# Reordering the second half-chunk of an attention + gated-MLP kernel: copies before masks, transposes and sums in twos

## The chip, the cores and the metric

The kernel runs on one core of a Trainium2 chip. The metric is the device time of one execution in microseconds (us), median of the runs shown. Beside it stands one execution taken by the hardware profiler, from which all durations in this document come. Engines are named as in the profile: PE (TensorE matmuls), PEld (TensorE weight loads), DVE (VectorE), ACT (ScalarE), POOL (GpSimd), SP (SyncE, which here only issues DMAs).

## What is computed

Attention with 4 batches, 8 heads, 768 positions and head dimension 64, followed by a gated MLP on 3072 tokens (512 to 1536 to 512). A query attends to the first 8 positions (global) and to the last 96 (local), with a bias that falls with the distance by a slope of its head:

```python
scores = scale * np.matmul(q, k.transpose(0, 1, 3, 2))
...
keep = is_global | is_local
dist = np.where(is_global & ~is_local, float(n_local), np.abs(rel).astype(np.float32))
slopes = 2.0 ** (-8.0 * (np.arange(H, dtype=np.float32) + 1) / H)
bias = -slopes[:, None, None] * dist[None, :, :]
scores = np.where(keep, scores + bias, -1000000000.0)
a = softmax(scores)
x = (a @ v), heads side by side, one row per token
out = (np.maximum(x @ w_gate, 0.0) * (x @ w_val)) @ w_out
```

(The softmax and the last two lines are shortened here.)

## The kernel before

**Half-chunks.** The work is cut into 8 half-chunks `s` of 384 queries (batch `s // 2`, half `s % 2`), and the 8 heads into 4 pairs `p`. A half-chunk has two parts: attention, which leaves a normalised `xT` (512 features by 384 tokens), and the MLP on it (`ffn_pieces`, L525 to L569). Half-chunks 0 and 1 are written out by hand, order and all (L621 to L734); later ones are woven (`weave`, L588), with attention of the next half-chunk between the MLP products of this one. The order that the code is written in is the order of each engine's queue, since scheduling is manual. This case concerns half-chunk 1 ("the second half", L690 to L734).

**Attention of a pair.** `piece_t` (L299) transposes the pair's keys and queries on PE into a PSUM bank of the pool `av_ps` (2 banks); in half-chunk 1 its matmuls fill 64 columns of the array each. `piece_copy` has DVE copy the result out: the keys in three instructions (L282, L283, L284), the queries in two (L315). Then scores are made on PE in three banks of the pool `qk_ps` (3 banks), in one of two ways:

- by bias (`piece_bias` L327, `piece_scores` L342, `piece_exp` L359): PE adds the distance bias as matmuls with `sid` and `dd`, and ACT takes the exp of a bank into an `es` buffer. Nothing is left for DVE.
- by mask (`piece_qk` L411): PE makes bare scores, ACT takes the exp (L414), and DVE multiplies the result by a ready-made mask exp(-slope x distance) (L423, five instructions for a pair in this half). The masks `m_all` are built per head by ACT (`setup_mask`, L245).

Half-chunk 0 uses the bias for all pairs; half-chunk 1 uses it for pairs 0 and 3 and the mask for pairs 1 and 2. An `es` buffer is one of three in rotation; for the last pair of half-chunk 0 the unused tile `kN` serves instead.

**Sums.** `piece_av_wide` (L474) makes, for a pair, the sums of the weights (with a matrix of ones) and the weighted sums of V, each with matmuls of 64 columns for one head and the other beside it. ACT takes Ln (L491) and Exp of its negative (L496) as the inverse, and DVE multiplies into `xT` (L502). `AV(s, p)` is all of this for one pair. It takes two PSUM banks, from `av_ps` or where named from another pool.

**V rows.** The 8 global V rows are copied on DVE beside each of the seven V tiles (`copy_v_globals`, L145): tiles 1 to 3 in half-chunk 0, tiles 4 to 6 in half-chunk 1.

**MLP.** `gate(fc)` is four matmuls of 384 columns (L525) into a bank of the pool `ff_ps` (3 banks, in rotation) and a relu on ACT (L534); `val(fc)` is four matmuls and a multiplication on DVE into `ht` (L541). While half-chunk 1's attention is made, gates and vals of half-chunk 0 are placed between its parts. Weights come by DMAs that POOL issues (L166), some of them while this goes on; POOL also issues the loads of q and k for half-chunk 2 (L111).

The order of half-chunk 1 before the change, from L690 on: transposes, copies and biased scores of pairs 0 and 1 as far as the copies; masks of heads 2 and 3; three gates; then `S1(1)` (QK, exps and masks of pair 1), masks 4 and 5, V rows 4 to 6, transposes and copies of pair 2, gate 3, transposes and copies of pair 3, val 0, `S1(2)`, val 1, sums of pair 0, bias and scores of pair 3, val 2, sums of pair 1, val 3, sums of pair 2, gate 4, sums of pair 3, val 4, gate 5, val 5. In this text val and gate with a number mean the block `fc`; the next product after val 5 is the first gate of half-chunk 1 ("chunk 1").

Of the kernel before, what the change touches and what calls it, by code (L numbers as in the profile page):

```python
# [15 lines left out]
def kernel(  # L16
# [21 lines left out]
    HP = H // 2  # L38
# [6 lines left out]
    NT = -(-S // KT)  # L45
# [43 lines left out]
    kNb = [const.tile([128, HP, QH], BF16, name=f"kN{i}") for i in range(2)]  # L89
# [53 lines left out]
    def copy_v_globals(eng, b, j0, j1):  # L143
        t = vbuf[b % 2][0:NG, :, D:].rearrange("p j (h z) -> p j h z", z=2 * D)[:, :, :, 0:D]
        eng.tensor_copy(t[:, j0:j1], t[:, 0:1].to_broadcast([NG, j1 - j0, H, D]))  # L145
# [98 lines left out]
    def setup_mask(h):  # L244
        nc.scalar.activation(m_all[:, h], dd, AF.Exp, bias=0.0, scale=-slopes[h])  # L245
# [42 lines left out]
    def piece_t(s, p, pool=av_psum, name="av_ps", apart=False):  # L288
        for i in (1, 0):
            if i == 1 or apart:  # L290
                tp = pool.tile([128, 512], FP32, name=name)
                tp = tp[:, 0:QH].bitcast(BF16).rearrange("d (i t) -> d i t", i=2)
            tp_of[s, p, i] = tp[:, i, :]
            for n in range(NN):
                for e in range(2 if s == 1 else 1):
                    r = slice(64 * e, 64 * e + 64) if s == 1 else slice(0, 128)
                    src = (qk16[s, i][:, 2 * p + e, n * D : (n + 1) * D] if s == 1
                           else cast_of[s, p][:, i, n])
                    nc.tensor.matmul(tp[r, i, n * 128 : (n + 1) * 128],  # L299
                                     lhsT=src, rhs=ident, is_transpose=True,  # L300
                                     start=((i == 1 or apart) and n == 0),
                                     stop=((i == 0 or apart) and n == NN - 1))

    def piece_copy_k(s, p):
        b, half = divmod(s, 2)
        put_keys(nc.vector.tensor_copy, nc.vector.tensor_copy, kT[b % 2][p], tp_of[s, p, 1], half)

    def piece_copy(s, p):
        piece_copy_k(s, p)
        piece_copy_q(s, p)  # L310
# [8 lines left out]
    def piece_bias(s, p):  # L319
        pool, name = (ff_psum, "ff_ps") if s == 0 and p % 2 else (qk_psum, "qk_ps")  # L320
        banks = [pool.tile([128, 512], FP32, name=name) for _ in range(3)]
        qk_of[s, p] = banks
        for g, bank in enumerate(banks_of_half[s % 2]):
            c = 0
            for i, (j, a, w, m) in enumerate(bank):
                for e in range(2):
                    nc.tensor.matmul(banks[g][:, c : c + NN * w], lhsT=sid[:, 2 * p + e],  # L327
                                     rhs=dd[:, 0 if j == 0 else 1, :, m : m + w],
                                     start=(i == 0 and e == 0), stop=False, skip_group_check=True)
                    c += NN * w  # L330
# [13 lines left out]
                c += n_  # L344

    def piece_exp(s, p, g):
        if s == 0 and p == HP - 1:

            es = kNb[0].rearrange("d p t -> d (p t)")[:, 480 * g : 480 * (g + 1)]
        else:  # L350
            if g == 0:
                es01_of[s, p] = es_pool.tile([128, 2, 480], BF16, name="es01")
            es = es01_of[s, p][:, g] if g < 2 else es_pool.tile([128, 480], BF16, name="es2")
        c = 0
        for j, a, w, m in banks_of_half[s % 2][g]:
            for e in range(2):
                es_of[s, p, j, e] = (es, c)
                c += NN * w
        nc.scalar.activation(es[:, 0:c], qk_of[s, p][g][:, 0:c], AF.Exp, bias=0.0, scale=scale)  # L359

    def piece_biased(s, p):
        piece_scores(s, p)
        for g in range(3):
            piece_exp(s, p, g)
# [30 lines left out]
        out += [(0.0, lambda p=p: piece_order(s, p)) for p in range(HP)]  # L395
        return out

    def piece_qk(s, p, g):
        b, half = divmod(s, 2)
        kt = kT[b % 2][p]  # L400
        qd = qTb[s % 2][:, p].rearrange("d e (n p) -> d e n p", n=NN)
        bank = banks_of_half[half][g]
        cols = sum(2 * NN * w for _, _, w, _ in bank)
        ps = qk_psum.tile([128, 512], FP32, name="qk_ps")
        if g == 0:
            es01_of[s, p] = es_pool.tile([128, 2, 480], BF16, name="es01")
        es = es01_of[s, p][:, g] if g < 2 else es_pool.tile([128, 480], BF16, name="es2")
        c = 0
        for j, a, w, m in bank:
            n_ = 2 * NN * w  # L410
            nc.tensor.matmul(ps[:, c : c + n_], lhsT=kt[:, j, :],  # L411
                             rhs=qd[:, :, :, a : a + w], start=True, stop=True)
            c += n_
        nc.scalar.activation(es[:, 0:cols], ps[:, 0:cols], AF.Exp, bias=0.0, scale=scale)  # L414
        c = 0
        for j, a, w, m in bank:
            n_ = 2 * NN * w
            e4 = es[:, c : c + n_].rearrange("k (e n p) -> k e n p", e=2, n=NN)
            mk = m_all[:, 2 * p : 2 * p + 2, 0 if j == 0 else 1, :, m : m + w]
            if w == WQ:  # L420
                e4 = e4.rearrange("k e n p -> k e (n p)")
                mk = mk.rearrange("k e n p -> k e (n p)")
            nc.vector.tensor_mul(e4, e4, mk)  # L423
            for e in range(2):
                es_of[s, p, j, e] = (es, c + e * NN * w)
            c += n_
# [35 lines left out]
    def piece_av_wide(s, p, *pools):  # L462

        b, half = divmod(s, 2)
        todo = [t for bank in banks_of_half[half] for t in bank]
        pools = pools or (AVB,)
        av = [pool.tile([128, 512], FP32, name=name) for pool, name in (pools[0], pools[-1])]
        for what in range(2):
            av3 = av[what][:, 0:QH].rearrange("d (n p) -> d n p", n=NN)
            for i, (j, a, w, m) in enumerate(todo):  # L470
                for e in range(2):
                    es, ce = es_of[s, p, j, e]
                    z0 = D + 2 * D * (2 * p + e)
                    nc.tensor.matmul(av3[64 * e : 64 * e + 64, :, a : a + w],  # L474
                                     lhsT=ones if what == 0 else vbuf[b % 2][:, j, z0 : z0 + D],
                                     rhs=es[:, ce : ce + NN * w].rearrange("k (n p) -> k n p", n=NN),
                                     start=(i == 0), stop=(i == len(todo) - 1),
                                     skip_group_check=True)
        av_of[s, p] = av
# [9 lines left out]
    def piece_ln_wide(s, p):  # L489
        ln = rc_pool.tile([128, QH], FP32, name="lnd")  # L490
        nc.scalar.activation(ln, av_of[s, p][0][:, 0:QH], AF.Ln, bias=0.0, scale=1.0)  # L491
        av_of[s, p, "l"] = ln

    def piece_inverse_wide(s, p):
        rc = rc_pool.tile([128, QH], FP32, name="rcp")
        nc.scalar.activation(rc, av_of[s, p, "l"], AF.Exp, bias=0.0, scale=-1.0)  # L496
        av_of[s, p, "r"] = rc

    def piece_mul_wide(s, p):
        if s not in xT_of:  # L500
            xT_of[s] = xt_pool.tile([128, N_DC, QH], BF16, name="xT")
        nc.vector.tensor_tensor(xT_of[s][:, p, :], av_of[s, p][1][:, 0:QH], av_of[s, p, "r"], op=ALU.mult)  # L502
# [102 lines left out]
    V, P, A = nc.vector, nc.gpsimd, nc.scalar  # L605
# [11 lines left out]
    def AV(s, p, *pools):  # L617
        piece_av_wide(s, p, *pools)
        piece_norm_wide(s, p)
# [11 lines left out]
    cast(0, 0, V, V)  # L631
    piece_t(0, 0, apart=True)
    piece_bias(0, 0)
    piece_copy_k(0, 0)
    piece_copy_q(0, 0, nc.scalar.copy)
    zero_keys()
# [18 lines left out]
    piece_bias(0, 3)  # L655
    copy_v_globals(V, 0, 1, 4)
    piece_biased(0, 3)
    piece_av_wide(0, 0, QKB)
    piece_sums_wide(0, 0)

# [5 lines left out]
    for j in range(4, NT):  # L666
        load_v(0, j)


    def S1(p):  # L670
        if p in (1, 2):
            for g in range(3):
                piece_qk(1, p, g)
        else:
            piece_bias(1, p)
            piece_biased(1, p)

    def TC(s, p, *pool):
        piece_t(s, p, *pool)
        piece_copy(s, p)  # L680
# [18 lines left out]
    piece_mul_wide(0, 2)  # L699
    piece_mul_wide(0, 3)  # L700
    piece_copy(1, 1)
    for h in (2, 3):
        setup_mask(h)
    piece_biased(1, 0)
    load_v(0, 3, 24)
# [5 lines left out]
        f(0, LAST)  # L711
    for f in gate[0:3]:
        f(LAST, N_DC)
    S1(1)
    for h in (4, 5):
        setup_mask(h)
    copy_v_globals(V, 0, 4, NT)
    TC(1, 2)
    gate[3]()
    TC(1, 3)  # L720
    val[0]()
    S1(2)
    val[1]()
    AV(1, 0)
    S1(3)
    val[2]()
    AV(1, 1)
    val[3]()
    AV(1, 2, QKB)
    F0[8]()  # L730
    AV(1, 3)
    F0[9]()
    F0[10]()
    F0[11]()  # L734
# [65 lines left out]
```

## Time and profile before

| | us |
|---|---|
| median of 4 runs | 248.23 (247.83 to 249.31) |
| the profiled execution | 247.89 |
| its span, first to last instruction | 246.1 |
| PE busy | 238.3 (97%) |
| ACT busy | 157.7 (64%) |
| DVE busy | 136.0 (55%) |
| POOL busy | 91.9 (37%) |
| chain that ended last, share of PE | 93% |
| mean granted TensorE clock | 0.999 |

The page cuts the span into 40 slices of 6.15 us. In a row of slices a digit is the busy share in tenths, and the row PEclk has the granted clock. The list of waits says which engine and line waited for which, with the sum, the number and the longest of the waits. The chain of work follows back from the last instruction what released each step: start, length, engine, tile and line. In the timeline a row is a start, a length, an engine, a line, and what was written from what. A busy PE is not a PE at its peak, since matmuls overlap and their ends are modelled; the prediction therefore uses the distances between starts.

### The profile page before, as it was taken

To read this page: it belongs to the slowest core of one execution; us is meant where nothing else is said; L and a number is where in the kernel's file an instruction comes from. 1 tells how busy PE (TensorE), PEld (TensorE's weight loads), DVE (VectorE), ACT (ScalarE), POOL (GpSimd) and SP (SyncE) were. 2 spreads that over 40 slices of the span, in tenths; PEclk is the share of its full clock that TensorE was granted. 3 is DMA by queue.
4 is the path that set the end of the run, shared out by engine and by line. 5 is a ranking of instruction groups with operands and counts; after the bars stand their busy time and mean duration, and the time that the engine had idled before them with its cause. 6 is when DMAs were issued, how large, how long until landed. Compare 5 with 4: busy or idle time off the path is not lost.

```text
span 246.1 us, 4852 instructions
## 1 busy us (share of the span) xinstructions
PE 238.3 (97%) x1739; PEld 143.8 (58%) x1739; DVE 136.0 (55%) x355; ACT 157.7 (64%) x329; POOL 91.9 (37%) x213
## 2 busy tenths in 40 slices
PE   8887999999999999999999999999999999999994
PEld 4674666666454666556655666556665666556644
DVE  6866766976531576335772567426763466523410
ACT  6997864377553877567774877567774778553311
POOL 8998924924680076202536064403620000000000
PEclk9999999999999999999999999999999999999999
DMA  5999999997699776838439967828441100020012
GB/s 183 183 175 183 208 290 232 144 105 247 144 166 174 235 116 152 91 92 253 105 89 96 272 149 151 79 99 257 93 101 73 58 0 3 6 109 17 0 42 87
DMA packets 76536, 32.35 MB, mean 131 GB/s; under 512 B 55424, under 2 KB 73216, under 8 KB 76512
## 3 DMA queue, kind: packets, MB, share of 16 engines
q0 software_dynamic: 34896, 10.27, 37.4%
q1 hardware_dynamic: 41616, 21.78, 33.1%
q8 instruction: 13, 0.21, 0.4%
q14 instruction: 11, 0.09, 0.1%
HBM read 28.38 MB, written 6.29 MB: 141 GB/s over the span
## 4 chain that ended last, share of the span: by engine, by line
PE 93%; DVE 3%; ACT 2%; issue 0%; DVEq 0%
PE ff_ps L525 50%; PE ff_ps L548 24%; PE qk_ps L411 6%; PE av_ps L439 6%; PE ff_ps L250 1%; PE ff_ps L563 1%; PE av_ps L299 1%; PE qk_ps L342 1%; PE av_ps L474 1%; PE qk_ps L327 1%; DVE qT L315 1%; PE qk_ps L299 1%; ACT kN L359 1%; DVE es L423 1%; ACT grelu L534 1%; DVE kT L278 0%
## 5 line engine op out<-in xcount | busy, mean ns | idle before, releaser
L525 PE MATMUL ff_ps<-xT,wv 128*128 128x384 bf16 x384 | 78.1, 326 | 0.0
L525 PE MATMUL ff_ps<-xT,wg 128*128 128x384 bf16 x384 | 77.7, 326 | 0.0
L534 ACT ACTIVATE grelu<-ff_ps 128x384 bf16<-128x384 f32 x96 | 46.8, 490 | 32.5 <-PE ff_ps L525 15.0
L541 DVE TENSOR_TENSOR ht<-ff_ps,grelu 128x384 bf16<-128x384 f32 x96 | 53.2, 555 | 22.6 <-PE ff_ps L525 21.0
L548 PE MATMUL ff_ps<-wo_sb,ht 128*128 128x512 bf16 x276 | 63.2, 379 | 0.5 <-DVE ht L541 0.5
L423 DVE TENSOR_TENSOR es<-es,m_all 128x432 bf16<-128x432 bf16 (+5 forms) x118 | 33.9, 317 | 35.9 <-ACT es L414 34.6
L525 PEld LDWEIGHTS <-wv 128*128 128x128 bf16 x384 | 36.3, 98 | 22.2 <-DMA wv<-in_moe_w_val_dram 0.2
L525 PEld LDWEIGHTS <-wg 128*128 128x128 bf16 x384 | 35.9, 98 | 22.1 <-issue 0.2
L414 ACT ACTIVATE es<-qk_ps 128x432 bf16<-128x432 f32 (+2 forms) x78 | 41.0, 532 | 9.5 <-PE qk_ps L411 7.2
L459 DVE TENSOR_TENSOR xT<-av_ps,rcp 64x384 bf16<-64x384 f32 x48 | 26.7, 555 | 33.9 <-ACT rcp L453 21.1
L548 PEld LDWEIGHTS <-ht 128*128 128x128 bf16 x276 | 26.0, 97 | 28.6 <-issue 0.6
L448 ACT ACTIVATE lnd<-av_ps 64x384 f32<-64x384 f32 x48 | 23.3, 485 | 13.3 <-PE av_ps L439 12.5
L367 POOL CAST kc<-ks 128x384 bf16<-128x384 f32 x20 | 9.5, 520 | 59.1 <-DMA ks<-in_k_dram 59.1
L553 ACT COPY osb<-ff_ps 128x512 f32<-128x512 f32 x23 | 13.5, 586 | 24.5 <-PE ff_ps L548 24.3
L411 PE MATMUL qk_ps<-qT,kT 128*128 128x432 bf16 (+5 forms) x118 | 26.5, 286 | 1.6 <-DVE qT L315 1.6
L149 POOL DMA_DIRECT2D vbuf<-in_v_dram x29 | 24.8, 862 | 0.0
L439 PEld LDWEIGHTS <-vbuf 128*128 128x128 bf16 x216 | 17.8, 98 | 6.4
L439 PE MATMUL av_ps<-es,vbuf 128*128 128x216 bf16 (+4 forms) x216 | 20.5, 226 | 0.0
L411 PEld LDWEIGHTS <-kT 128*128 128x128 bf16 x118 | 11.4, 98 | 9.9 <-DVE qT L315 2.0
L375 POOL CAST qz<-qs 128x192 bf16<-128x192 f32 x40 | 12.9, 370 | 3.5 <-DMA qs<-in_q_dram 3.5
L453 ACT ACTIVATE rcp<-lnd 128x384 f32<-128x384 f32 x24 | 12.5, 523 | 0.8
L282 POOL COPY kT<-kN 128x240 bf16<-128x240 bf16 x12 | 5.2, 431 | 5.1 <-DMA kN<-kc 5.1
(105 smaller groups left out, 154.7 us busy)
## 6 DMA issues: line engine op xcount, KB each, us to landing
out_dram<-osb SPq DMA_DIRECT2D x23, 256.0 KB
ks<-in_k_dram SPq DMA_DIRECT2D x5, 768.0 KB
qs<-in_q_dram SPq DMA_DIRECT2D x5, 768.0 KB
vbuf<-in_v_dram POOLq DMA_DIRECT2D x23, 120.0 KB, 4.7
wv<-in_moe_w_val_dram POOLq DMA_DIRECT2D x3, 512.0 KB, 10.5
wo_sb<-in_moe_w_out_dram POOLq DMA_DIRECT2D x1, 1536.0 KB, 22.5
wg<-in_moe_w_gate_dram POOLq DMA_DIRECT2D x2, 512.0 KB, 10.5
ks<-in_k_dram SPq DMA_DIRECT2D x4, 192.0 KB
```

Source lines behind the costliest of these rows:

```text
L149: nc.gpsimd.dma_start(out=v_dst(b, NG + r0, NG + r0 + n, j), in_=v[b, :, KT * j + r0 : KT * j + r0 + n, :].rearrange("h p d -> p h d"))
L411: nc.tensor.matmul(ps[:, c : c + n_], lhsT=kt[:, j, :], rhs=qd[:, :, :, a : a + w], start=True, stop=True)
L414: nc.scalar.activation(es[:, 0:cols], ps[:, 0:cols], AF.Exp, bias=0.0, scale=scale)
L423: nc.vector.tensor_mul(e4, e4, mk)
L439: nc.tensor.matmul(av3[:, :, a : a + w], lhsT=vb[:, j, z0 : z0 + 128], rhs=es[:, c : c + NN * w].rearrange("k (n p) -> k n p", n=NN), star ...
L448: nc.scalar.activation(ln[o0 : o0 + 64], av[d0 : d0 + 64, 0:QH], AF.Ln, bias=0.0, scale=1.0)
L459: nc.vector.tensor_tensor(xT_of[s][r, p, :], av_of[s, p, e][r, 0:QH], av_of[s, p, "r"][r], op=ALU.mult)
L525: nc.tensor.matmul(st[key][:, 0:QH], lhsT=w_of(w, dc, fc), rhs=xT_of[c][:, dc, :], start=(dc == 0), stop=(dc == N_DC - 1))
L534: nc.scalar.activation(gr, psg[:, 0:QH], AF.Relu, bias=0.0, scale=1.0)
L541: nc.vector.tensor_tensor(ht[:, fc, :], psv[:, 0:QH], st["r", fc], op=ALU.mult)
L548: nc.tensor.matmul(ps2, lhsT=ht[:, fc, n * 128 : (n + 1) * 128], rhs=wo_sb[:, fc, :], start=(fc == 0), stop=(fc == N_FC - 1))
L553: nc.scalar.copy(osb, ps2)
```

## The change

In half-chunk 1: the transposes of pairs 2 and 3 are made together, ahead of QK of pair 1; the mask multiplications of pairs 1 and 2 are put off (`piece_qk` collects them in a list, the new `piece_mask` issues one) until after the copies of pairs 2 and 3, and after val 1; bias and scores of pair 3 come ahead of the sums of pair 0; the sums of pairs 0 and 1, and of 2 and 3, stand together, with the steps of the two pairs interleaved on ACT and DVE. V rows of tiles 4 to 6 are copied in half-chunk 0. The mask of head 2 is built at the start, those of 3 and 4 where 2 and 3 were, that of 5 behind the exps of pair 1. The exps of pair 3 go into `kN` as in half-chunk 0.

```diff
-        if s == 0 and p == HP - 1:
+        if p == HP - 1:
-            es = kNb[0].rearrange("d p t -> d (p t)")[:, 480 * g : 480 * (g + 1)]
+            es = kNb[s].rearrange("d p t -> d (p t)")[:, 480 * g : 480 * (g + 1)]
...
-    def piece_qk(s, p, g):
+    def piece_qk(s, p, g, later=None):
...
+        if later is None:
+            piece_mask(s, p, bank, es)
+        else:
+            later.append(lambda: piece_mask(s, p, bank, es))
+
+    def piece_mask(s, p, bank, es):
...
     piece_bias(0, 0)
+    setup_mask(2)
     piece_copy_k(0, 0)
...
     piece_biased(0, 3)
+    copy_v_globals(V, 0, 4, NT)
     piece_av_wide(0, 0, QKB)
...
-    for h in (2, 3):
+    for h in (3, 4):
         setup_mask(h)
...
-    S1(1)
-    for h in (4, 5):
-        setup_mask(h)
-    copy_v_globals(V, 0, 4, NT)
-    TC(1, 2)
+    piece_t(1, 2)
+    piece_t(1, 3)
+    masks = {p: [] for p in (1, 2)}
+    for g in range(3):
+        piece_qk(1, 1, g, masks[1])
+    setup_mask(5)
+    piece_copy(1, 2)
     gate[3]()
-    TC(1, 3)
+    piece_copy(1, 3)
+    for g in range(3):
+        piece_qk(1, 2, g, masks[2])
+    for f in masks[1]:
+        f()
     val[0]()
-    S1(2)
+    piece_bias(1, 3)
+    piece_biased(1, 3)
     val[1]()
-    AV(1, 0)
-    S1(3)
+    piece_av_wide(1, 0)
+    piece_ln_wide(1, 0)
+    piece_av_wide(1, 1, QKB)
+    piece_inverse_wide(1, 0)
+    for f in masks[2]:
+        f()
+    piece_ln_wide(1, 1)
+    piece_mul_wide(1, 0)
+    piece_inverse_wide(1, 1)
     val[2]()
-    AV(1, 1)
+    piece_mul_wide(1, 1)
     val[3]()
-    AV(1, 2, QKB)
     F0[8]()
-    AV(1, 3)
+    piece_av_wide(1, 2)
+    piece_ln_wide(1, 2)
+    piece_av_wide(1, 3, QKB)
+    piece_inverse_wide(1, 2)
+    piece_ln_wide(1, 3)
+    piece_mul_wide(1, 2)
+    piece_inverse_wide(1, 3)
+    piece_mul_wide(1, 3)
     F0[9]()
     F0[10]()
     F0[11]()
```

(`F0[8]` to `F0[11]` are gate 4, val 4, gate 5 and val 5.)

More of the change, by code (lines that the diff above doesn't have):

```diff
@@ L667 @@
         load_v(0, j)
[L670 to L676, printed above, removed]
     def TC(s, p, *pool):
```

## The prediction, made before the changed kernel had run

> **What bounds the kernel now.** First the page's busy rows and its slices:
>
> ```profile
> PE 238.3 (97%) x1739; PEld 143.8 (58%) x1739; DVE 136.0 (55%) x355; ACT 157.7 (64%) x329; POOL 91.9 (37%) x213
> PE   8887999999999999999999999999999999999994
> PEclk9999999999999999999999999999999999999999
> ```
>
> PE is full at full granted clock from slice 4 on (a slice is 6.15 us). Whatever the change brings must come out of slices 0 to 3. The waits over the whole span, PE alone, name what can be had there:
>
> ```profile
> PE qk_ps L411 <- DVE qT L315: 1.6, 1, 1.6
> PE ff_ps L250 <- DVE warm L188: 1.0, 1, 1.0
> PE ff_ps L342 <- DVE qT L315: 0.9, 2, 0.5
> PE av_ps L299 <- ACT lnd L491: 0.6, 1, 0.6
> PE ff_ps L548 <- DVE ht L541: 0.5, 1, 0.5
> ```
>
> One stall of 1.6 us is the largest, and it lies in the second half of attention (after L690). The chain of work in 17 to 36 us shows what it waited for:
>
> ```profile
> 17.99 1.64 PE ff_ps L525 x10
> ...
> 20.91 0.47 ACT es L414
> 21.38 0.02 issue
> 21.41 1.27 DVE es L423 x5
> 22.68 0.59 DVE vbuf L145
> 23.27 0.03 issue
> 23.30 0.41 DVE kT L282
> ...
> 24.25 0.37 DVE qT L315
> 24.62 0.05 issue
> 24.67 0.77 PE qk_ps L411 x5
> ```
>
> DVE, first in first out, does five masks of pair 1 and a V-row copy before it copies the transposes of pair 2, for which PE waits. From 24.67 the chain is PE alone; the next wait of PE is the 0.5 at 61.5. So a saving made before 34 us reaches the end, unless it meets a transfer that lands at a fixed time.
>
> **The change, part by part.** The matmuls stay the same in number and size. I replay the new order with starts of single instructions from narrow windows of the timeline. Steps from start to start: product of four matmuls 0.65; a QK pair (five L411) 0.60; bias 0.62 in three banks; ACT exp 0.45 for 480 columns and 0.41 for 432, mask build 0.45, relu 0.37; DVE copies of a pair 1.35, five masks 1.19, ht 0.48; an engine sees another's result after 0.04.
>
> *Copies first.* The gates end at 19.78 as before. Transposes (1,2) start at 19.87 (their q rows landed at 11.90+7.7=19.6), both pairs are through at 20.67, and DVE, idle since 19.45, copies pair 2 from 20.43 to 21.75 and pair 3 to 23.1. QK of pair 1 is 20.67 to 21.27, gate 3 to 21.92, and QK of pair 2 starts at 21.92, its qT ready at 21.75. The 1.8 us between starts (22.86 to 24.67) is gone.
>
> *What is late next: ACT.* All 3 qk_ps banks turn over with exps. ACT's row: exps of pair 1 at 21.07, 21.54, 21.99; mask 5 at 22.40; relu 3 at 22.85; exps of pair 2 at 23.23, 23.68, 24.13, each ending 0.57 to 0.60 after its start. PE's waits for banks: QK of pair 2, second bank 0.07, third 0.22; it ends at 22.78, val 0 at 23.43. The bias of pair 3 wants the banks that pair 2's exps empty: 0.43 until 23.86, 0.24 until 24.32, 0.19 until 24.73. Together 1.15 us of new stall. The scores run 24.91 to 25.51 (kT at 23.1 in time), val 1 to 26.16.
>
> *Transposes and sums in twos.* A change between 128-column and 64-column matmuls costs PE time: L525 to L474 at 26.01 is 0.095 beyond streaming, L474 to L327 at 26.76 is 0.105. Before: six stretches of 64 columns after 19.78 (two of transposes, four of sums); after: three. Saved 3 x 0.20 = 0.6, part of it in the stall. [...]
>
> *Sums 0 and 1, vals, sums 2 and 3.* Sums 0 and 1 from 26.26 to 27.62; val 2, val 3 and gate 4 to 29.57 (its weights landed at 19.66+8.6=28.26). DVE: masks of pair 1 by 24.3, val 0's ht 24.3, val 1's ht not before 26.35. This ht is the new wait in DVE's queue: the masks of pair 2, mul 0, val 2's ht and mul 1 are queued behind it, and masks of pair 2 end at 28.1. Sums of pair 2 want them at 29.67: hidden by 1.6 us. Sums 2 and 3 run to 31.03, then val 4 (L525), gate 5, val 5 end at 32.98. ACT's inverse of pair 3 ends at 32.24, mul 3 follows until 32.83, and val 4's ht until 33.29. Chunk 1's first gate takes the ff_ps slot of val 4, so PE waits 0.35 and starts at 33.33. Before, that gate started at 34.43: **gain 1.10**.
>
> *V rows 4 to 6 copied in the first half.* One DVE copy, 0.67, at 12.42 to 13.09, in a hole that the row "DVE xT L502 <- ACT rcp" shows as 1.94 until 14.41: zero; if that cover were gone, 0.67. [...] By the row next to this: the same copy at 11.74 lay beside POOL issues of 0.785 and 0.792 (0.77 elsewhere), at 22.59 beside one of 0.874, so at most 0.1. Zero either way in the sum.
>
> *Mask 2 at the start.* One ACT exp between the sids (end 3.73) and the qT copies at 4.93 on the opening chain. Its input is complete at 4.38 (POOL L236), so it starts at 4.42 and lets ACT go at 4.87: zero. Upper bound, input seen only when PE first reads it at 4.69: ACT free at 5.14, 0.21 late, all of it on the chain. Below zero is excluded, the copy waits for PE. I take 0.05. In its place masks 3 and 4 are built where 2 and 3 were; mask 4 leaves the place before relu 3, counted above.
>
> *Spare buffer.* The last exps write kN; a third es buffer is not awaited. kN is next written after 58 us: zero. Without the spare they would wait for sums 0, 27.6 instead of 25.3, and the masks' slack would shrink by that.
>
> POOL and SP keep their orders in the built program; no DMA is moved.
>
> Sum: 1.10 - 0.05 = 1.05. The profiled execution took 247.89 (span 246.1 and 1.8 around it), so 246.84; the median shown is 0.34 higher, 248.23, and the change there gives **247.2**, or -0.4%. Measurement can tell some 0.5%, 1.24 us, from no change.
>
> **Rivals.**
> *A, the stall only moves (0.20).* ACT's row of eight instructions from 21.07 to 24.69 replaces DVE's. [...]
> *B, most of the stall really goes (0.17).* [...]
> *C, slower (0.07): descriptors.* DVE is now busy without a break from 20.43 to 24.3, beside POOL's issues of wv and wg at 20.42, 21.16 and 22.44. If POOL were held until 24.3, wv would land 3.9 later, at 34.8, and val 4 would wait from 31.0: 3.8 less 0.35, against the gain of 1.05, so +2.4: 250.6. It turns to a loss when wv lands after 32.4. Against it: POOL issues of 21.16 beside masks and of 23.74 to 25.5 beside copies from PSUM show no such stretch (0.77, 0.90; the one of 25.5, beside nothing but such copies, 1.04 for three times the bytes).
> That the change does not do what it says is excluded by the built order of DVE and PE.
>
> **How the numbers follow.** Likeliest (0.56): gain 0.7 to 1.35, that is 246.9 to 247.5 by itself. Range 246.4 to 248.3: it takes in B and A and leaves out C and tails. Faster by over 0.5% (gain above 1.24): B's 0.17 and 0.13 of the likeliest, 0.30. Slower: C, 0.07. The rest, 0.63, within 0.5%.
>
> **What would show it.** PE's wait for DVE qT before QK of pair 2 gone; in its place waits of PE for ACT es at bias and QK, 1.15 in all and each under 0.5; a wait for ht of about 0.35 at chunk 1's first gate; that gate at 33.3 to 33.4; the opening qT copy at 4.93 to 5.0; val 4 without a DMA wait. A wait on wv or wg over 0.4, an opening chain later by over 0.2, or a new PE wait after 34 us would make it wrong.

## The result and the profile after

| | before | after |
|---|---|---|
| median of the runs beside each other | 247.94 (64 runs) | 247.50 (43 runs) |
| ratio, with its 95% interval | | 0.9980 (0.9973 to 0.9987) |
| the profiled execution | 247.89 | 247.27 |
| its span | 246.1 | 245.5 |
| end of the last matmul | 243.00 | 242.38 |

The changed kernel is 0.50 us faster (0.32 to 0.67), 0.2%: within what was called no change. The time of 247.5 lies near the forecast of 247.2, but the gain is half of the 1.05 forecast. Where the other half went is the subject of what follows.

The page of the changed kernel, in the rows shown of before:

```profile
PE 237.8 (97%) x1739; PEld 143.5 (58%) x1739; DVE 136.3 (56%) x355; ACT 157.7 (64%) x329; POOL 92.0 (37%) x213
...
PE   7889999999999999999999999999999999999994
...
PEclk9999999999999999999999999999999999999999
```

Slices 2 and 3 of PE (counted from 0) went from 8 and 7 to 8 and 9 tenths; from there on there is nothing that a tenth can show. Slice 0 reads 7 for 8, but the first gate starts at 17.81 for 17.83: the opening lost nothing. The waits of PE over the whole span of the changed kernel (sum, number, longest):

```profile
PE qk_ps L342 <- ACT qT L315: 0.6, 1, 0.6
...
PE ff_ps L342 <- DVE qT L315: 0.6, 2, 0.4
PE ff_ps L554 <- DVE ht L547: 0.4, 1, 0.4
PE qk_ps L327 <- ACT es L414: 0.3, 1, 0.3
...
PE ff_ps L531 <- DVE ht L547: 0.2, 1, 0.2
```

(From L417 on, a line of before stands 6 lower in after: L525 is now L531.) The 1.6 us for qT ahead of L411 is gone. The ACT wait at L327 that stands in its place was forecast. The last row was not: it lies at 49.7 us, in a stage that the change does not touch. The timeline of PE in the stage that it does touch (start, length, what, and in brackets the idle time and who ended it):

```profile
20.65 0.77 PE L411 MATMUL qk_ps<-qT,kT 128*128 128x144 bf16 x5
21.25 0.81 PE L531 MATMUL ff_ps<-xT,wg 128*128 128x384 bf16 x4
21.90 1.01 PE L411 MATMUL qk_ps<-qT,kT 128*128 128x144 bf16 x5
22.75 0.81 PE L531 MATMUL ff_ps<-xT,wv 128*128 128x384 bf16 x4
23.86 1.23 PE L327 MATMUL qk_ps<-dd,sid 128*128 128x72 bf16 x10 [0.30 <-ACT es L414]
24.93 0.76 PE L342 MATMUL qk_ps<-qT,kT 128*128 128x144 bf16 x5
```

The prediction had 20.67, 21.27, 21.92, 22.78, 23.86 and 24.91 for these starts, and 33.33 for chunk 1's first gate, which came at 33.32. So up to 34 us the replay held to a few hundredths.

The span divides at three starts that every kernel here has: the first gate of half-chunk 0, chunk 1's first gate, and the first output product (L548 before, L554 after), which is behind a stretch of 27 us that is the same code in both:

| trace | gate 0 to chunk 1's first gate | to the first output product | to the end of the last matmul |
|---|---|---|---|
| before | 16.60 | 27.54 | 181.03 |
| after | 15.51 | 28.02 | 181.04 |

The first stretch gained 1.09; the second, unchanged in code, gave back 0.48. Within it PE's distances between starts, less the time the columns take to stream (in after, from 34.62 to 39.17, each of seven products of four matmuls of 384 columns starts 0.65 after the one before it), show three waits in after (two in before): at 47.88 us 0.22 (0.09 before), at 49.74 us 0.39 (none before), and at the first output product 0.60 (0.63 before). 0.13 + 0.39 - 0.03 = 0.49.

**The wait at 49.74.** The timeline of after around it:

```profile
49.13 1.02 DVE L547 TENSOR_TENSOR ht<-ff_ps,grelu 128x384 bf16<-128x384 f32 x2
49.17 0.35 PE L411 MATMUL qk_ps<-qT,kT 128*128 128x432 bf16 x1
...
49.74 0.48 PE L531 MATMUL ff_ps<-xT,wg 128*128 128x384 bf16 x2 [0.22 <-DVE ht L547]
```

and the same place in before:

```profile
50.11 0.56 DVE L541 TENSOR_TENSOR ht<-ff_ps,grelu 128x384 bf16<-128x384 f32 x1
50.15 0.35 PE L411 MATMUL qk_ps<-qT,kT 128*128 128x432 bf16 x1
...
50.34 0.49 PE L525 MATMUL ff_ps<-xT,wg 128*128 128x384 bf16 x2
```

In both, DVE is behind with its ht product, since it copies transposes ahead of it. In before the gate starts all the same, 0.33 us before that product ends (50.67). In after it starts only when the first of the two ht products has ended (49.69). The gate needs no ht: it needs a bank of `ff_ps`. The two built programs differ here in one choice: the pool gave this gate the bank that a relu on ACT had left in before, and in after the bank that this ht product was reading. Up to this tile, the 45th of the pool, both kernels have the same sequence of banks; from it on, two of the three are exchanged.

**The wait at 47.88.** DVE came late to this one too. The timeline of after:

```profile
45.93 1.80 POOL L149 DMA_DIRECT2D vbuf<-in_v_dram  x2
...
46.23 0.60 DVE L280 COPY kT<-kT 128x56 bf16<-128x56 bf16 x1
46.33 0.91 DVE L315 COPY qT<-qk_ps 64x384 bf16<-64x384 bf16 x2
```

The copy within kT takes 0.18 in three of its four instances of half-chunk 2 in before (the fourth, beside a POOL cast, took 0.31), and 0.60 here: it ends at 46.84, and the first of the two POOL issues at 46.83. The same copy in before, and the POOL issue beside it:

```profile
47.41 0.18 DVE L280 COPY kT<-kT 128x56 bf16<-128x56 bf16 x1
```

```profile
47.28 0.90 POOL L149 DMA_DIRECT2D vbuf<-in_v_dram  x1
```

There it began 0.13 us into the issue, here 0.30; the last section has more cases.

### The profile page after: what moved, and what is told of

Its sections match the earlier page's. It is cut to its first block, busy times and chain, and to the rows that moved or that the text cites. A ratio compares the mean times of both kernels' runs of the same rounds, so it can differ in the third digit from the quotient of the medians.

```text
span 245.5 us, 4850 instructions
## 1 busy us (share of the span) xinstructions
PE 237.8 (97%) x1739; PEld 143.5 (58%) x1739; DVE 136.3 (56%) x355; ACT 157.7 (64%) x329; POOL 92.0 (37%) x213
## 4 chain that ended last, share of the span: by engine, by line
PE 74%; DVE 1%; ACT 1%; issue 0%; DVEq 0%
PE ff_ps L531 38%; PE ff_ps L554 24%; PE av_ps L445 5%; PE qk_ps L411 5%; PE ff_ps L569 1%; DVE xT L465 0%; DVE ht L547 0%; ACT rcp L459 0%; DVE es L429 0%; ACT lnd L454 0%; ACT grelu L540 0%; DVE osb L574 0%; DVEq L574 0%
## 5 line engine op out<-in xcount | busy, mean ns | idle before, releaser
L531 PE MATMUL ff_ps<-xT,wg 128*128 128x384 bf16 x384 | 77.7, 326 | 0.4 <-DVE ht L547 0.2
L531 PE MATMUL ff_ps<-xT,wv 128*128 128x384 bf16 x384 | 77.9, 326 | 0.0
L554 PE MATMUL ff_ps<-wo_sb,ht 128*128 128x512 bf16 x276 | 63.2, 379 | 0.4 <-DVE ht L547 0.4
L429 DVE TENSOR_TENSOR es<-es,m_all 128x432 bf16<-128x432 bf16 (+5 forms) x118 | 34.4, 322 | 34.5 <-ACT es L414 33.1
L531 PEld LDWEIGHTS <-wv 128*128 128x128 bf16 x384 | 36.4, 98 | 22.3 <-issue 0.2
L531 PEld LDWEIGHTS <-wg 128*128 128x128 bf16 x384 | 36.0, 97 | 22.9 <-issue 1.1
L554 PEld LDWEIGHTS <-ht 128*128 128x128 bf16 x276 | 26.0, 97 | 28.6 <-issue 0.5
L411 PE MATMUL qk_ps<-qT,kT 128*128 128x432 bf16 (+5 forms) x118 | 26.7, 286 | 0.1
L411 PEld LDWEIGHTS <-kT 128*128 128x128 bf16 x118 | 11.4, 98 | 8.1
L278 POOL COPY kT<-kN 128x360 bf16<-128x360 bf16 x8 | 4.3, 537 | 8.4 <-DVE xT L465 5.0
## 6 DMA issues: line engine op xcount, KB each, us to landing
wv<-in_moe_w_val_dram POOLq DMA_DIRECT2D x3, 512.0 KB, 10.3
wg<-in_moe_w_gate_dram POOLq DMA_DIRECT2D x2, 512.0 KB, 10.3
```

The source lines that it names most:

```text
L411: nc.tensor.matmul(ps[:, c : c + n_], lhsT=kt[:, j, :], rhs=qd[:, :, :, a : a + w], start=True, stop=True)
L531: nc.tensor.matmul(st[key][:, 0:QH], lhsT=w_of(w, dc, fc), rhs=xT_of[c][:, dc, :], start=(dc == 0), stop=(dc == N_DC - 1))
L554: nc.tensor.matmul(ps2, lhsT=ht[:, fc, n * 128 : (n + 1) * 128], rhs=wo_sb[:, fc, :], start=(fc == 0), stop=(fc == N_FC - 1))
```

## The experiments

Theory T1: the stage before 34 us gained 1.1 as forecast; of that, 0.39 went to the bank of one gate and 0.13 to the held copy. R1: the rest of the gain meets something that ends at a fixed time, so a wait taken away earlier comes back later. R2: the opening (the mask of head 2) cost the missing half. The ratio is taken to the runs of before made beside each kernel; it is not the ratio of the two medians. "A", "B" and "C" are the three stretches of the table above, from each kernel's trace: one execution each.

| | median (runs) | ratio to before, interval | A | B | C |
|---|---|---|---|---|---|
| after | 247.50 (43) | 0.9980, 0.9973 to 0.9987 | 15.51 | 28.02 | 181.04 |
| e1, bank of after put back | 246.85 (5) | 0.9946, 0.9931 to 0.9962 | 15.51 | 27.41 | 181.04 |
| e2, bank of before exchanged | 248.34 (13) | 1.0018, 0.9998 to 1.0038 | 16.60 | 27.76 | 181.04 |
| e3, kT copy on ACT | 247.31 (8) | 0.9964, 0.9951 to 0.9978 | 15.50 | 27.74 | 181.04 |
| e4, e1 and e3 | 247.21 (13) | 0.9970, 0.9958 to 0.9983 | 15.50 | 27.78 | 181.04 |
| e5, masks at once | 249.17 (12) | 1.0039, 1.0023 to 1.0056 | 18.42 | 27.55 | 181.04 |
| e6, sums singly | 247.22 (6) | 0.9958, 0.9945 to 0.9972 | 15.66 | 27.29 | 181.04 |
| e7, V rows in the second half | 246.90 (4) | 0.9950, 0.9934 to 0.9965 | 15.51 | 27.29 | 181.04 |
| e8, val 1 ahead | 246.61 (7) | 0.9948, 0.9928 to 0.9968 | 14.55 | 27.67 | 181.14 |
| e9, no spare buffer | 247.88 (10) | 0.9988, 0.9970 to 1.0005 | 16.47 | 27.38 | 181.04 |
| e10, mask 2 not at the start | 247.05 (10) | 0.9956, 0.9939 to 0.9973 | 15.51 | 27.79 | 181.14 |
| e11, V issues ahead of casts | 247.88 (10) | 0.9976, 0.9954 to 0.9997 | 15.66 | 28.03 | 181.56 |
| e12, e8 and a second bank | 247.06 (11) | 0.9949, 0.9929 to 0.9969 | 14.55 | 26.83 | 182.22 |

Medians of before: 248.21 (28 runs) beside e1 to e4, 248.03 (22) beside e5 to e8, 248.13 (34) beside e9 to e12.

### e1 and e2: the bank alone

The pool of three banks becomes three pools of one, and a list of 228 digits says which bank each tile takes. e1 is after with the list of before; e2 is before with the list of after.

```diff
-    ff_psum = ctx.enter_context(tc.tile_pool(name="ffps", bufs=3, space=bass.MemoryType.PSUM))
+    ff_banks = [ctx.enter_context(tc.tile_pool(name=f"ffps{i}", bufs=1, space=bass.MemoryType.PSUM))
+                for i in range(3)]
+    ff_order = iter(
...
+    class ff_psum:
+        @staticmethod
+        def tile(shape, dtype, name):
+            return ff_banks[int(next(ff_order))].tile(shape, dtype, name=name)
```

> The changed kernel, all orders kept; only the PSUM bank of one tile is other: the gate of block 8 of half-chunk 0 (the first product behind QK of half-chunk 2, at 49.74 in the changed kernel's trace) gets the bank that a relu on ACT has left, as before the change, and not the one that an ht product on DVE still holds until 49.69; the two banks stay exchanged from there on. Theory T1 (the stage before 34 us gained 1.1 as forecast, and some 0.5 is given back at 47 to 50 us, 0.37 of it by this bank): PE's idle time before that gate (0.22 by idle, 0.39 beyond streaming) is gone, nothing takes its place, and the kernel is 0.35 us faster than the changed one, 0.9 below the kernel before. Rival R1 (the rest of the gain meets something later that ends at a fixed time, so a stall taken away at 50 us returns): the time stays 0.5 below the kernel before, and a later wait grows by 0.35. Rival R2 (the mask at the start or the opening costs the missing half): the time stays, as nothing at 50 us is to blame.

(Counted by products, the gate is that of block 9; block 8's gate and val come ahead of QK. The expectations say 8.)

> The kernel before, all orders kept; the same gate gets the bank that DVE's ht product holds (as in the changed kernel), and the two banks stay exchanged from there on. T1: that ht ended at 50.67 in the trace of before and the gate started at 50.33, so the gate starts at 50.72 and the kernel is 0.35 to 0.39 us slower than before. R1 and R2: no difference over 0.1.

The timeline of e1 at this gate:

```profile
49.23 0.56 DVE L558 TENSOR_TENSOR ht<-ff_ps,grelu 128x384 bf16<-128x384 f32 x1
49.27 0.35 PE L422 MATMUL qk_ps<-qT,kT 128*128 128x432 bf16 x1
...
49.46 0.49 PE L542 MATMUL ff_ps<-xT,wg 128*128 128x384 bf16 x2
```

The gate starts 0.19 after the QK product with DVE's ht (until 49.79) still running: the wait is gone. e2 is the mirror: the gate of before, which waited for nothing, now waits 0.39 (PE's two waits of 40 to 65 us in e2):

```profile
PE ff_ps L559 <- DVE ht L552: 0.3, 1, 0.3
PE ff_ps L536 <- DVE ht L552: 0.2, 1, 0.2
```

So 0.39 of the 0.48 is the bank, shown in both directions by the traces. That the pool is written as three pools is not the cause: e11, written so too but with the list of after, keeps the wait of 0.39. The times agree in sign: e1 is 1.34 below before (0.94 to 1.71); e2 is 0.45 above, but its interval takes in zero (0.05 below to 0.94 above). Both traces have a further 0.13 to 0.16 less at the first output product (0.47 instead of 0.60 and 0.63): DVE's mask multiplication ahead of it took 0.38, and 0.52 and 0.55 in after and before. POOL's casts lay beside it in all four, but in after and before it began 0.06 and 0.03 us into a cast, in e1 and e2 0.28 and 0.25 into one, and there the next cast was the longer one (0.58 and 0.55, for 0.50 in after and before). This looks like the held copy in another place, and is chance between traces as far as these show. R2 is out: the gain came back with nothing done to the opening. R1 is out at this size of gain.

### e3 and e4: the copy within kT on ACT

```diff
-            copy_small(kt[:, :, 0:NG], kt[:, 0:1, NG : 2 * NG].to_broadcast([128, NT, NG]))
+            (copy_globals or copy_small)(kt[:, :, 0:NG], kt[:, 0:1, NG : 2 * NG].to_broadcast([128, NT, NG]))
```

(`copy_globals` is ACT's copy in half-chunk 2 and absent elsewhere.)

> The changed kernel with its banks as they are; only the copy of the eight global keys within kT (L280) of half-chunk 2, four instructions at 42.4 to 48.3, goes from DVE to ACT. T1: the DVE copy that took 0.605 instead of 0.178 at 46.23, with the query copy after it 0.18 longer, is gone from DVE, so the ht that PE awaited at 47.88 is ready in time (0.13 less), and DVE is some 0.1 earlier per pair, so that the ht at 49.69 ends at 49.2 to 49.3 and the wait of the gate for it is halved or gone as well: 0.2 to 0.5 us faster than the changed kernel. If ACT is as late with the copy as DVE was, scores of half-chunk 2 do not ask for it before 49: no cost. R1: no difference.

> Both edits on the changed kernel: the gate of block 8 with the bank that the relu has left, and the copy of the global keys of half-chunk 2 on ACT. T1: both waits of 47.88 and 49.74 are gone, PE runs from 33.3 to 61 us without a wait, and the kernel is 1.0 to 1.1 us below the kernel before, which is the whole gain of the stage before 34 us. R1: 0.5 to 0.6 below the kernel before, with a later wait longer by as much.

e3 is 0.40 faster than after by the two ratios, within its 0.2 to 0.5. Both old waits are gone (none beyond 0.1 at 47.9 or 49.7, in e3 even with the bank of after, because DVE is earlier), and a new one has come: PE's waits of e3 in 40 to 60 us, then ACT's timeline at that place.

```profile
PE ff_ps L543 <- ACT grelu L552: 0.3, 1, 0.3
```

```profile
48.07 0.24 ACT L291 COPY kT<-kT 128x56 bf16<-128x56 bf16 x1 [1.12 <-DVE kT L289]
48.21 0.86 ACT L552 ACTIVATE grelu<-ff_ps 128x384 bf16<-128x384 f32 x2
```

ACT stands 1.12 us at the head of its queue for DVE's first key copy, with a relu behind it; a val of PE waits for that relu's bank, 0.45 (0.38 in e4). The expectation of e4, 1.0 to 1.1 below before, fell: 0.74 (0.42 to 1.04). It had asked when the scores want the copy, not what is queued behind a waiting copy on ACT.

### e5: the masks at once

e5 to e10 all have the bank of e1.

```diff
-        piece_qk(1, 1, g, masks[1])
+        piece_qk(1, 1, g)
...
-        piece_qk(1, 2, g, masks[2])
+        piece_qk(1, 2, g)
```

> The changed kernel with the bank of the first run (e1), and the masks of pairs 1 and 2 multiplied at once behind their exps again, ahead of the copies of pairs 2 and 3; transposes, sums in twos, V rows and buffer as changed. T1: DVE copies pair 2 behind five masks (until 22.6 or so) and not from 20.43, its qT is ready at 23.9 instead of 21.77, and QK of pair 2 starts some 2.1 us later; up to 0.3 of it comes back at the wait for ht ahead of chunk 1's first gate. So 1.7 to 2.2 us slower than e1, 0.8 to 1.3 slower than the kernel before. If the putting off of the masks is worth only the stall of 1.6 less the 1.15 that ACT takes in its place, it is 0.5 slower than e1.

PE's waits of e5 in 17 to 36 us, and its clock by stretches (length, busy, matmuls, clock as a share of full, DMA share, GB/s):

```profile
PE qk_ps L422 <- DVE qT L326: 2.3, 1, 2.3
```

```profile
22.00:24.40 2.40, 0.23 (x2) 1.00 2.12 171
24.40:25.60 1.20, 1.12 (x9) 1.00 1.28 203
25.60:29.00 3.40, 3.40 (x20) 0.51 1.25 209
29.00:32.00 3.00, 3.00 (x50) 0.99 1.23 205
```

QK of pair 2 starts 2.4 us later than in e1 (24.48 after transposes at 20.02; 22.10 after 20.06), for T1's 2.1. The half clock for 3.4 us was not expected. It fits that e5's runs fall in two groups: six with a mean clock of 0.998 to 1.0 at 248.11 to 248.89, six at 0.991 to 0.993 and 249.45 to 250.22. The profiled execution is of the second, so 1.7 of the 2.91 that its A is longer than e1's is the clock. The first group's middle, 248.45, is 1.6 above e1's median, just under T1's 1.7, and 0.4 above the median of before beside it, under the 0.8 to 1.3 forecast: e1 itself had come out faster than that sum assumed. The rival's 0.5 is out.

### e6: sums singly

```diff
     piece_av_wide(1, 0)
     piece_ln_wide(1, 0)
-    piece_av_wide(1, 1, QKB)
     piece_inverse_wide(1, 0)
...
     val[2]()
+    piece_av_wide(1, 1, QKB)
...
     val[3]()
+    piece_av_wide(1, 2)
...
     F0[8]()
-    piece_av_wide(1, 2)
...
```

> The changed kernel with the bank of e1, and the sums of half-chunk 1 singly again: sums 0, val 2, sums 1, val 3, sums 2, gate 4, sums 3, each with its Ln, inverse and multiplication behind it. Four stretches of 64 columns instead of two. T1, by 0.2 a stretch: val 4 starts 0.4 later than in e1 (13.5 us after gate 0 to 2 end, not 13.1 less), chunk 1's first gate 0.15 to 0.4 later, since Ln and inverse of pair 2 are then out of the way of pair 3's; 0.15 to 0.4 slower than e1. [...] If changes of width are free: equal to e1 or faster.

From the transposes to val 4: 11.65 us (31.55 - 19.90), against 11.20 in e1 (31.26 - 20.06). Two stretches more cost 0.45, 0.23 each, for the 0.20 forecast. Only 0.15 of it reaches chunk 1's first gate, where the wait for ht of 0.31 is gone. With sums singly before and in twos after, this part of the change is worth 0.15, not the 0.4 forecast for its two stretches; the times (0.3 above e1, intervals overlapping) cannot resolve it.

### e7: V rows in the second half

```diff
-    copy_v_globals(V, 0, 4, NT)
     piece_av_wide(0, 0, QKB)
...
     setup_mask(5)
+    copy_v_globals(V, 0, 4, NT)
```

> The changed kernel with the bank of e1, but the V rows of tiles 4 to 6 copied in half-chunk 1, on DVE ahead of the copies of pair 2 (in the first half not at all). T1: the copy of 0.59 to 0.67 stands on the path: qT of pair 2 at 22.4 instead of 21.77, QK of pair 2 0.4 to 0.5 later (0.22 of waiting for a bank is then inside it), and all behind it as late: 0.35 to 0.6 slower than e1. Rival (ACT's row of exps sets the pace, DVE has room): under 0.2.

A miss: A is 15.51, as in e1. DVE's timeline shows why:

```profile
19.48 0.68 DVE L156 COPY vbuf<-vbuf 8x1536 bf16<-8x1536 bf16 x1
20.44 0.41 DVE L293 COPY kT<-av_ps 128x240 bf16<-128x240 bf16 x1 [0.28 <-PE av_ps L310]
```

Once the masks no longer stand ahead of it, the copy falls into DVE's hole before the transposes are made. Moving the V rows was worth nothing beside the putting off of the masks.

### e9 and e10: spare buffer, mask at the start

```diff
-        if p == HP - 1:
+        if s == 0 and p == HP - 1:
```

> The changed kernel with the bank of e1, but the exps of pair 3 of half-chunk 1 go into an es buffer in rotation, not into kN. T1: that buffer is pair 0's and is free only when sums 0 end (26.9 in the changed kernel's times), so the exps of pair 3 start at 26.95 and not at 25.34, Ln of pair 0 is queued behind them, and sums 1, which take two banks that these exps empty, wait some 0.7: chunk 1's first gate 0.5 to 0.9 later than in e1. Rival (the buffer in rotation is no bound, as the kernel before shows, where no wait for it is seen): under 0.1.

PE's waits of e9 in 17 to 36 us:

```profile
PE qk_ps L491 <- ACT es L370: 0.6, 1, 0.6
PE qk_ps L338 <- ACT es L425: 0.3, 1, 0.3
```

The first is new, at 27.67, where sums 1 want the banks of the late exps. A is 0.96 longer than in e1, above the forecast's 0.9: without the buffer almost the whole of the 1.09 is gone.

```diff
-    setup_mask(2)
     piece_copy_k(0, 0)
...
-    for h in (3, 4):
+    for h in (2, 3, 4):
```

> The changed kernel with the bank of e1, but the mask of head 2 is built with those of heads 3 and 4 (at 17.2 us), not at the start. T1: the mask at the start lies in a hole of ACT (it ends at 4.85, the copy of qT waits for PE until 4.76 to 4.93), so the first scores of half-chunk 0 (5.77) move by 0.1 at most, and the third mask at 17.2 delays only exps that nobody awaits before 20.8: under 0.1 either way. If the mask at the start costs the missing part of the gain: 0.1 to 0.3 faster than e1.

The first scores start at 5.94 without the mask ahead of them (5.96 in before), and at 5.76 to 5.91 with it, in after and in every experiment that has it but e5 (6.38): no cost. B of this trace is 0.38 longer than e1's: two copies within kT were long (0.52 beside a cast, 0.61 beside an issue), and PE waited 0.51 at 48.44.

### e11: V issues ahead of the casts

The changed kernel with its own banks:

```diff
+    load_v_half(2)
     for p in range(HP):
         cast(2, p, P, P)
-    load_v_half(2)
```

> The changed kernel with its own banks; only POOL's issues of the V rows of half-chunk 2 go ahead of POOL's casts of q and k of half-chunk 2, into the time in which POOL waits for these to land (32.1 to 38.2). In all runs so far the DVE copy within kT took 0.178 when it began 0.05 to 0.26 us into such an issue, and until the issue's end when it began 0.30 to 0.72 into it. T1: without issues beside them the copies of half-chunk 2 take 0.18 (up to 0.34 beside a cast), so the wait at 47.88 (0.22 beyond streaming) shrinks to 0.1; that of the gate behind QK of half-chunk 2 (0.39, its bank) stays. 0.1 to 0.15 faster than the changed kernel, if the casts, which now come after 7 us of issues, are still in time for the transposes at 41.3; if they are not, PE waits there by as much as they are late.

The wait at 47.9 is gone and the 0.39 at the gate stands, as expected. But nothing is gained: the transposes of half-chunk 2 lose 0.21 to a cast, and 0.49 is lost at 72.96, the place that e12 explains. Val 4 also waits 0.24 for its weights, which land late in this trace alone, ahead of the place of the edit. The waits moved; the copy is no free saving.

### e8 and e12: a better version

e8 puts val 1 ahead of bias of pair 3 and gate 5 ahead of val 4; e12 also gives the first output product the bank that a relu has left (two digits exchanged in the list from there on).

```diff
     val[0]()
+    val[1]()
     piece_bias(1, 3)
     piece_biased(1, 3)
-    val[1]()
...
-    F0[9]()
     F0[10]()
+    F0[9]()
```

> A version that may beat both: the changed kernel with the bank of e1, val 1 ahead of bias of pair 3 (it fills the time in which PE waits for the exps of pair 2) and gate 5 ahead of val 4 (the weights of val 4 land at 30.9 us). T1 has the rest of the stall at ACT, 0.9 us at bias of pair 3, and 0.3 at the ht ahead of chunk 1's first gate: 0.65 and 0.3 can go, so chunk 1's first gate starts 0.4 to 0.95 earlier than in e1; the first transposes of half-chunk 2 then still come after their casts. 0.3 to 0.9 faster than e1, up to 2.0 below the kernel before. Rival: the weights of gate 4 (landed at 28.26) or of val 4 hold PE, and less than 0.2 is left.

A falls by another 0.96, the upper end: 0.65 of waits at bias of pair 3 and 0.31 at the ht are gone. 0.33 of it comes back at the first output product, where PE's wait of e8 in 58 to 75 us is now

```profile
PE ff_ps L565 <- DVE ht L558: 0.6, 1, 0.6
```

(0.80 beyond streaming), and the time is that of e1 within its interval: the 0.3 to 0.9 forecast is not seen there.

> The version of e8 with one more bank exchanged: the first output product of half-chunk 0 (the wait of 0.5 to 0.8 us at 61 us that every kernel so far has, for an ht product on DVE) gets the bank that the relu of the last gate has left. T1, by the same reading as in e1: that wait goes down to 0.1, nothing new takes its place, and it is 0.4 to 0.7 us faster than e8, 1.8 to 2.2 below the kernel before. Rival (the product needs ht itself, not only a bank): no difference.

Half right. The wait is gone and B falls to 26.83; PE, then ACT in 40 to 75 us and 58 to 75 us, and SP's own timeline show where the gain went:

```profile
PE av_ps L456 <- DVE es L440: 1.0, 1, 1.0
```

```profile
ACT osb L570 <- DMA out_dram<-osb: 2.2, 1, 2.2
```

```profile
63.49 3.77 SPq L393 DMA_TRANSPOSE qT<-qz  x2
67.37 0.52 SPq L571 DMA_DIRECT2D out_dram<-osb  x1
67.93 1.31 SPq L393 DMA_TRANSPOSE qT<-qz  x1
69.34 1.50 SPq L571 DMA_DIRECT2D out_dram<-osb  x2
```

The first output row is in its buffer at 63.1, but SP issues its DMA at 67.4, behind the transposes of half-chunk 3. The third output copy wants that buffer back and holds ACT until 69.9; an exp, its mask and a sum stand behind it. This is R1's mechanism, at 70 us. The time is not quite a fixed one: in e8 the two transposes began at the same 63.5 and the DMA was issued at 66.2, since they took 2.6; here the second took 2.49 and not the 1.31 of every other trace. Why is open, and so is how often: this execution took 246.33, against a median of 247.06. e1, e7, e8 and e12 are all 1.2 to 1.3 below before by their ratios, and these runs do not separate them; 1.8 to 2.2 was forecast for e12.

## Why the prediction was right in time and wrong in gain

- **What bounds the kernel, the replay, ACT as the next limit: right.** The stall of 1.6 is gone and the waits for ACT's exps are 0.22 at QK and 0.46, 0.26 and 0.21 at bias, 1.15 in all, as forecast. Chunk 1's first gate is at 33.32 for 33.33, its wait for ht 0.31 for 0.35.
- **Changes of width: right in price** (0.23 a stretch for 0.20, e6), but in the sum two of the three stretches were worth 0.15, since a wait for ht takes back the rest.
- **V rows at zero, mask at the start at 0.05: right in size** (e7, e10). e7 adds that the V rows would have cost nothing in the second half either, in another hole of DVE.
- **Spare buffer: right with it, wrong about its lack.** The prediction had only the masks' slack shrink without it. e9 shows 0.96, through sums 1, whose two banks the late exps empty. Since e5 and e9 each undo most of the gain or more, the parts of the change do not add up.
- **The step that failed: "So a saving made before 34 us reaches the end, unless it meets a transfer that lands at a fixed time."** It was read off the waits of before, where none lies between 34 and 61.5. But no wait is not the same as slack: at 50.3 a gate started 0.33 us ahead of the end of an ht product, and only because its bank was another. The new order let the pool hand out the other bank, 0.39 (e1, e2), and the shifted phase put a DVE copy into a POOL issue, 0.13. The prediction itself named a new PE wait after 34 us as what would make it wrong.
- **The rivals.** A, that the stall only moves: half of the gain was lost, but to a bank and a held copy, not to a transfer that lands at a fixed time. Such losses exist in other traces (val 4 of e11, the output rows of e12). The 480-column exps of half-chunk 1 began 0.45 to 0.47 apart in after, for the 0.45 of the replay. B, that most of the stall really goes: the 1.15 came whole, with bias waits that are not shorter, and a change of width was not much dearer than forecast (0.23 a stretch, e6). So no run shows the longer exps or the dearer changes that the ends of the range allowed for. C: wv for val 4, issued at 20.35 in after, landed 10.3 us later, and val 4 started at 31.06 with no wait for it; before it was issued at 20.42 and landed after 10.5, at 30.92.
- **Luck.** The time of 247.5 lies in the likeliest band, 246.9 to 247.5, but the gain of 0.50 lies below that band's 0.7 to 1.35. The forecast time stood on the 4 runs of before at 248.23; the 64 runs give 247.94, from which the same gain leads to 246.9. An error of 0.55 in the gain so became one of 0.3 in the time.

What stays open is how often executions without a profile meet held copies. e1 is 0.84 below after by the two ratios; its trace shows 0.61, of which 0.39 is the bank.

## What to carry to other kernels

When an order is changed, compare not only the order of the instructions but also, for each product further on, which bank its tile gets and which engine it waits for: one exchange cost here a third of the gain, 15 us behind the edit. A trace without waits says nothing of slack, so ask at each later place by how much the producer is early. Before a step is moved to an engine with room, ask what is queued behind it there while it waits.

## What the runs showed of the chip that was not expected

- **DVE and POOL, held by phase.** In the traces up to e8, a DVE copy within SBUF (128x56 bf16, 0.18 at its shortest) that started 0.05 to 0.26 us into a POOL issue of 0.90 to 0.94 took 0.18 (in before at 47.41, in an issue from 47.28; in after at 44.36, in one from 44.10). One that started 0.30 to 0.72 into it ended with the issue, within 0.02 us of it, and so took up to 0.60 in after and 0.61 in e10 (in after from 46.23 to 46.84, in an issue from 45.93 to 46.83, and from 48.30 to 48.63, in one from 47.72 to 48.62). Copies from PSUM beside the same issues kept their length, unless they stood behind a held one: in after the first key copy took 0.52 for each of the four pairs of half-chunk 2, the two query copies 0.71 for three of them and 0.91 behind the copy of 46.23. The issue itself was not longer in either case: 0.90 beside the copy of 46.23 in after, 0.90 beside that of 47.41 in before.

  Here POOL started first and held DVE, but not for the whole of its issue: a copy that started up to 0.26 us into it passed.

- **A pause of PE and its clock.** In the profiled execution of e5, PE waited 2.3 us, up to 24.48. The granted clock was 1.00 from 24.4 to 25.6, 0.51 from 25.6 to 29.0 and 0.99 from 29.0 to 32.0, its mean over the execution 0.992; five more of its twelve runs have a mean of 0.991 to 0.993. From 22.0 to 25.6, ahead of the fall, PE was busy for 1.35 us of the 3.6. In the profiled execution of before, with its pause of 1.6, the clock was 1.00 from 22.5 to 28.0. But before shows a mean clock of 0.991 to 0.993 in 3 of the 84 runs beside the experiments, at 249.84 to 250.06; in the changed kernel and the experiments with the masks put off it never fell below 0.998. So the change seems also to take away a rare loss of some 1.8 us, which a median does not show; none of those runs of before has a profile, so that the pause is its cause is not shown. Why only half of the runs of e5 show the low clock, no run here tells.
